# Late stages wholly in program order, and the O*wo stage's loads reordered: wo's last rows first, its third O^T tile ungated

## The chip, the cores and the metric

One core of one Trainium2 chip. The metric is the time of one execution in device microseconds (us). Single executions of one kernel differ by some 20 us here (see the ranges below); in the profiled runs nearly all of that comes from when the attention stage ends. So beside the median of several runs I use a second measure that does not carry that scatter: the **stage start**, the time in one profiled run from row 0's first matmul of the O*wo stage to row 4's first.

## The reference, cut to what matters

```python
def _fwd_reference(A_x, ...):
    xn = _layernorm(A_x)
    s = A(xn, k_cache, v_cache, wq, wo)    # 32 heads of attention, then O @ wo
    g = _silu(B(xn, w_gate, w_up, w_down)) # sigmoid-gated MLP
    return A_x + s * g                     # S = 2048 rows, D = 576

def reference(...):                        # the output and the gradients of all inputs but B_x
    out, vjp = jax.vjp(_fwd_reference, ...)
    return (out, *vjp(grad_out))
```

The product `O @ wo` is the stage that this study is about. It takes some 140 us of 4930.

## The kernel before: the parts that matter

A row block of the stage is 128 rows. Its operand is an O^T tile: SP's transposing load of 128 rows of O for all 32 heads (1.05 MB). Three such tiles are used in turn: `oTs[0]` lies over the attention's KQ, `oTs[1]` over xnT, `oTs[2]` over xn_all. Of wo's rows those of 23 heads (`h_early`) are in SBUF by the time the stage begins; those of nine (`h_late`) go into Kn, Vn and dOn, which the attention uses to its end.

```python
with late("pc") as pc, late("pcf") as pcf, \
        tc.manual_schedule(engines={SP, Pool, DVE, PE}):     # ScalarE is left to the scheduler
    # ...
    def row_loads(st):                    # GpSimd: three loads of 144 KB for row block st
        res = []
        for nm, src in (("dsg", dsg_d), ("g2b", g2_d), ("xb", x2)):
            t_ = ldp3.tile([P, D], bf, name=nm)
            nc.gpsimd.dma_start(t_[:], src[st * P:(st + 1) * P, :])
            res.append(t_)
        return res

    R0 = min(3, NT)
    loads = {}
    loads[0] = row_loads(0)
    for st in range(1, R0):
        if st > 1:                        # the gate: one element of oTs[2] <- row 0's xb
            nc.gpsimd.tensor_copy(oTs[st][0:1, 0, 0:1], loads[0][st % 3][0:1, 0:1])
        load_oT(oTs[st], st)              # SP: dma_start_transpose
    for view, h0, n, dead in wo_parts:
        if dead in (1, 2, 3):
            load_wo_rows(view, h0, 0, n)  # GpSimd: Kn, Vn, dOn, 432 KB each
    for st in range(1, R0):
        loads[st] = row_loads(st)
    # ...
    def close(st):                        # after row block st's last matmul
        accs = accs_of.pop(st)
        dsg, g2b, xb = loads.pop(st)
        if st + R0 < NT:
            load_oT(oTs[st % 3], st + R0)          # SP
            loads[st + R0] = row_loads(st + R0)    # GpSimd: does not wait for SP
        # ... ScalarE: s_sb <- accs; VectorE: doB <- s_sb*dsg, xb <- s_sb*g2b + xb
        nc.gpsimd.dma_start(o0[st * P:(st + 1) * P, :], xb[:])

    for st in range(R0 - 1):
        mm(st, h_early)
    for st in range(NT):
        # ... turn_do: TensorE transposes doB of an earlier row block
        mm(st, h_late if st in accs_of else h_early + h_late)
        close(st)
        if st == 0 and R0 > 1:
            mm(R0 - 1, h_early)
```

Row 3's O^T tile (KQ again) can only be issued when row 0 has closed. Row 3's three loads stand on GpSimd behind those of row 2, and nothing ties them to row 0's close.

## Time and profile before

| | before |
|---|---|
| median of the first three runs (range) | 4933.09 us (4931.61 to 4936.69) |
| profiled run, span | 4929.9 us, mean granted TensorE clock 0.998 |
| TensorE busy | 98% of the span; the chain that ended last is 94% TensorE |
| stage start, 3533.59 to 3577.50 | 43.9 us |
| from row 4's first matmul to the end | 1352.4 us |

The page says that TensorE is the limit, and the timeline says where TensorE stands still. The lines that carry this are in the prediction below. In all views PE is TensorE's matmuls, PEld its weight loads, DVE VectorE, ACT ScalarE, POOL GpSimd and SPq the transfers that SP issues.

### The profile page before, as it was taken

To read this page: it belongs to the slowest core of one execution; us is meant where nothing else is said; L and a number is where in the kernel's file an instruction comes from. 1 tells how busy PE (TensorE), PEld (TensorE's weight loads), DVE (VectorE), ACT (ScalarE), POOL (GpSimd) and SP (SyncE) were. 2 spreads that over 40 slices of the span, in tenths; PEclk is the share of its full clock that TensorE was granted. 3 is DMA by queue.
4 is the path that set the end of the run, shared out by engine and by line. 5 is a ranking of instruction groups with operands and counts; after the bars stand their busy time and mean duration, and the time that the engine had idled before them with its cause. 6 is when DMAs were issued, how large, how long until landed. Compare 5 with 4: busy or idle time off the path is not lost.

```text
span 4929.9 us, 100847 instructions
## 1 busy us (share of the span) xinstructions
PE 4835.4 (98%) x40273; PEld 2894.6 (59%) x41029; DVE 2802.5 (57%) x6554; ACT 2472.1 (50%) x4228; POOL 840.7 (17%) x1329
## 2 busy tenths in 40 slices
PE   9999999999999999999999999999899999999998
PEld 4445666666666666666666666666555555555554
DVE  4544666666666666656656666665434555554215
ACT  4431766766676676666667667667312111111111
POOL 3322111111111111111111111111221111111112
PEclk9999999999999999999999999999999999999999
DMA  7886999999999999999999999999999999998665
GB/s 260 274 201 170 225 227 231 215 227 230 227 232 224 230 227 227 233 221 233 223 224 228 232 226 223 232 229 224 225 221 234 230 232 225 226 224 213 187 173 153
DMA packets 3045845, 1097.11 MB, mean 223 GB/s; under 512 B 2949553, under 2 KB 2953778, under 8 KB 3045362
## 3 DMA queue, kind: packets, MB, share of 16 engines
q1 hardware_dynamic: 2946594, 771.07, 83.5%
q0 software_dynamic: 98160, 318.85, 20.5%
q8 instruction: 323, 5.29, 0.4%
q14 instruction: 160, 1.31, 0.1%
q10 hardware_dynamic: 608, 0.59, 0.0%
HBM read 175.31 MB, written 177.93 MB: 72 GB/s over the span
## 4 chain that ended last, share of the span: by engine, by line
PE 94%; DMA 2%; DVE 2%; issue 1%; ACT 1%; SPq 0%; POOL 0%; POOLq 0%; ACTq 0%; DVEq 0%
PE acc L683 18%; PE acc L744 18%; PE acc L998 13%; PE acc L1054 8%; PE dp L706 8%; PE sp L636 8%; PE acc L215 6%; PE u_ps L450 3%; PE dh L1111 3%; PE g_ps L448 3%; PE acc L533 3%; PE acc L958 2%; PE acct L145 1%; DMA dST<-Pq 1%; DVE Pq L709 1%
## 5 line engine op out<-in xcount | busy, mean ns | idle before, releaser
L654 ACT ACTIVATE Pq<-sp 128x1024 bf16<-128x1024 f32 x1024 | 1047.1, 1023 | 267.3 <-PE sp L636 224.3
L709 DVE SCALAR_TENSOR_TENSOR Pq<-dp,negdelta,Pq 128x1024 bf16<-128x1024 f32 x512 | 655.2, 1280 | 46.6 <-PE dp L706 45.2
L712 ACT ACTIVATE t<-dp,negdelta 128x1024 bf16<-128x1024 f32 x512 | 567.1, 1114 | 214.7 <-PE dp L706 165.3
L683 PEld LDWEIGHTS <-dST 128*128 128x128 bf16 x8192 | 508.2, 98 | 152.1 <-DMA dST<-Pq 11.0
L706 PE MATMUL dp<-VT,dOT 128*128 128x512 bf16 x1919 | 581.6, 379 | 2.4
L683 PEld LDWEIGHTS <-PT 128*128 128x128 bf16 x8192 | 500.1, 98 | 130.9 <-DMA PT<-Pq 11.1
L636 PE MATMUL sp<-KQ 128*128 128x512 bf16 x1858 | 568.9, 380 | 5.2 <-issue 5.2
L683 PE MATMUL acc<-Kn,dST 128*128 128x128 bf16 x8192 | 557.1, 219 | 8.8 <-DMA dST<-Pq 6.9
L683 PE MATMUL acc<-Vn,PT 128*128 128x128 bf16 x8192 | 542.1, 219 | 8.5 <-DMA PT<-Pq 6.2
L744 PE MATMUL acc<-Pq,dOn 128*128 128x512 bf16 x1983 | 527.3, 379 | 10.0
L713 DVE TENSOR_TENSOR Pq<-t,Pq 128x1024 bf16<-128x1024 bf16 x512 | 354.5, 692 | 316.7 <-ACT t L712 306.9
L744 PE MATMUL acc<-Pq,Qn 128*128 128x512 bf16 x2013 | 524.3, 380 | 4.9
L724 ACT ACTIVATE dq_n<-acc,rsc 128x128 bf16<-128x128 f32 x512 | 187.5, 366 | 333.7 <-PE acc L683 312.0
L1154 DVE TENSOR_TENSOR dxn<-acc,dxn 128x576 f32<-128x576 f32 x272 | 206.1, 758 | 247.8 <-PE acc L1054 247.8
L744 PEld LDWEIGHTS <-Qn 128*128 128x128 bf16 x2048 | 200.4, 98 | 240.9 <-issue 1.6
L744 PEld LDWEIGHTS <-dOn 128*128 128x128 bf16 x2048 | 198.8, 98 | 233.8
L1116 ACT ACTIVATE ndh<-dh 128x512 bf16<-128x512 f32 x144 | 86.0, 597 | 452.8 <-DVE du_blk L1114 449.0
L636 PEld LDWEIGHTS <-KQ 128*128 128x128 bf16 x2048 | 179.3, 98 | 127.7 <-issue 7.2
L641 DVE TENSOR_REDUCE rs_all<-rsp 128x1 f32<-128x2 f32 x512 | 78.5, 153 | 306.5 <-ACT Pq L654 295.0
L706 PEld LDWEIGHTS <-dOT 128*128 128x128 bf16 x2048 | 178.8, 98 | 124.4 <-issue 11.9
L677 POOL DMA_DIRECT2D on_d<-o_n x128 | 97.1, 759 | 778.8 <-DVE junk L695 447.8
L677 POOL DMA_DIRECT2D dq_d<-dq_n x128 | 97.9, 765 | 719.7 <-ACT dq_n L724 679.8
(208 smaller groups left out, 6794.4 us busy)
## 6 DMA issues: line engine op xcount, KB each, us to landing
out_dram<-kvn POOLq DMA_DIRECT2D x64, 512.0 KB, 4.7
ah<-a_d POOLq DMA_DIRECT2D x18, 1024.0 KB, 9.2
ah<-h_d POOLq DMA_DIRECT2D x18, 1024.0 KB, 12.1
h_d<-h_row POOLq DMA_DIRECT2D x64, 256.0 KB, 3.5
a_d<-a_row POOLq DMA_DIRECT2D x64, 256.0 KB, 3.8
x_all<-in_A_k_cache_dram SPq DMA_DIRECT2D x64, 256.0 KB, 3.8
on_d<-o_n POOLq DMA_DIRECT2D x128, 128.0 KB, 4.4
kvT_d<-KQ POOLq DMA_DIRECT2D x32, 512.0 KB, 5.3
```

The lines of the kernel that those rows point to most:

```text
L215: nc.tensor.matmul(av[:, :CH], lhsT=w[:, i, :], rhs=srcT[:, i, cs], start=(i == 0), stop=(i == DT - 1))
L636: nc.tensor.matmul(sp[:, c * CH:(c + 1) * CH], lhsT=hs.QT[:, qt * P:(qt + 1) * P], rhs=hs.KT[:, hf * HW_ + c * CH: hf * HW_ + (c + 1) * CH ...
L654: nc.scalar.activation(Pq[:, hsl], sp[:], AF.Exp, scale=SCALE, accum_out=hs.rsp[:, hf:hf + 1])
L683: nc.tensor.matmul(hs.acc[:, 0, :], lhsT=T[:, kt, :], rhs=rhs[:, kt, :], start=(kt == 0), stop=(kt == NT - 1))
L706: nc.tensor.matmul(dp[:, c * CH:(c + 1) * CH], lhsT=hs.dOT[:, qt * P:(qt + 1) * P], rhs=hs.VT[:, hf * HW_ + c * CH: hf * HW_ + (c + 1) * C ...
L709: nc.vector.scalar_tensor_tensor(Pq[:, hsl], dp[:], hs.negdelta[:, qt:qt + 1], Pq[:, hsl], op0=ALU.add, op1=ALU.mult)
L712: nc.scalar.activation(t[:], dp[:], AF.Identity, bias=hs.negdelta[:, qt:qt + 1], scale=1.0)
L713: nc.vector.tensor_tensor(Pq[:, hsl], t[:], Pq[:, hsl], op=ALU.mult)
L744: nc.tensor.matmul(self.acc, lhsT=self.nat[:, qt, :], rhs=self.slabs[qt][:, cs], start=(qt == self.lo), stop=(qt == self.hi - 1))
L998: nc.tensor.matmul(acc[:, n0:n0 + nn], lhsT=lhs[:, st, cols], rhs=rhs[:, st, n0:n0 + nn], start=(st == 0), stop=(st == NT - 1))
L1054: nc.tensor.matmul(acc[:, n0:n0 + nn], lhsT=lT, rhs=w[:, n0:n0 + nn], start=(k == 0), stop=(k == len(terms) - 1))
L1154: nc.vector.tensor_tensor(dxn[:, st, :], acc[:, :D], dxn[:, st, :], op=ALU.add)
```

## The change

Its intent: take away TensorE's three waits at the start of the O*wo stage (7.4 us, and the half clock after them). The copy that gates the transpose into xn_all goes. The last rows of wo are issued ahead of row 0's loads, Kn, whose slab is read longest, as the last of the three. ScalarE, so far left to the scheduler in these stages, runs in program order too.

```diff
-            tc.manual_schedule(engines={SP, Pool, DVE, PE}):      # names shortened
+            tc.manual_schedule():
@@
-            h_late = [h0 + k for _, h0, n, dead in wo_parts if dead in (1, 2, 3) for k in range(n)]
+            h_late = [h0 + k for _, h0, n, dead in sorted(wo_parts, key=lambda w: w[3] == 1) if dead in (1, 2, 3) for k in range(n)]
@@
             loads = {}
-            loads[0] = row_loads(0)
             for st in range(1, R0):
-                if st > 1:
-                    nc.gpsimd.tensor_copy(oTs[st][0:1, 0, 0:1], loads[0][st % 3][0:1, 0:1])
                 load_oT(oTs[st], st)
-            for view, h0, n, dead in wo_parts:
+            for view, h0, n, dead in sorted(wo_parts, key=lambda w: w[3] == 1):
                 if dead in (1, 2, 3):
                     load_wo_rows(view, h0, 0, n)
+            loads[0] = row_loads(0)
             for st in range(1, R0):
                 loads[st] = row_loads(st)
```

## The prediction

> **What bounds the kernel now.** I read the page first: PE (TensorE) is busy 98% of the 4929.9 us, and the chain that ended last is 94% PE. So nothing but TensorE's own gaps, its clock, and the tail after its last matmul can be won. Then I listed what TensorE waited for after 3490 us: its matmuls waited 14.5 us in sum, and about half of that stands in one place, the start of the O*wo stage (L958, 3533 to 3675 us). The third view is the timeline of that start (start us, us, engine and line, what it writes <- reads, count, [idle before <- releaser]):
>
> ```profile
> 3533.59 4.33 PE L958 MATMUL acc<-dsT,KQ 128*128 128x512 bf16 x33
> 3534.85 0.55 POOL L756 DMA_DIRECT2D kvT_d<-VT  x1 [1.81 <-DVE VT L754]
> ...
> 3540.22 0.18 POOL L942 COPY xn_all<-xb 1x1 bf16<-1x1 bf16 x1 [3.21 <-DMA xb<-in_A_x_dram]
> 3540.43 7.27 SPq L584 DMA_TRANSPOSE xn_all<-on_d  x1
> 3540.72 0.76 POOL L575 DMA_DIRECT2D Kn<-in_A_wo_dram  x1 [0.31 <-issue]
> ...
> 3547.80 1.60 PE L958 MATMUL acc<-Kn,KQ 128*128 128x512 bf16 x6 [2.77 <-DMA Kn<-in_A_wo_dram]
> 3547.80 0.10 PEld L958 LDWEIGHTS <-KQ 128*128 128x128 bf16 x1 [2.87 <-issue]
> ...
> 3552.16 0.10 PEld L958 LDWEIGHTS <-KQ 128*128 128x128 bf16 x1 [2.87 <-issue]
> ...
> 3556.34 0.14 PEld L958 LDWEIGHTS <-xn_all 128*128 128x128 bf16 x2 [1.67 <-issue]
> ...
> 3569.38 4.33 PE L958 MATMUL acc<-dsT,KQ 128*128 128x512 bf16 x33
> ...
> 3577.50 2.83 PE L958 MATMUL acc<-dsT,xnT 128*128 128x512 bf16 x20
> ```
>
> A row block of this stage is 32 heads of two matmuls; 23 heads' rows of wo ("early") are already there, 9 ("late": Vn, dOn, Kn) are loaded only now. The order on TensorE is: row 0 early, row 1 early, row 0 late, row 2 early (its O^T tile is xn_all), row 1 late, row 2 late, row 3. The reader should see that SP's transpose into xn_all and GpSimd's wo loads both start only at 3540.4 to 3540.7. The reason is L942, a one-element copy which waits for row 0's xb load. TensorE finishes the two early parts at 3544.9 and then waits three times, 2.87, 2.87 and 1.67 us.
>
> The fourth view is the same stretch in windows (us; then busy time and count of PE, PEld, DVE, ACT, POOL; granted clock, DMA share, GB/s):
>
> ```profile
> 3542.00:3544.00 2.00, 1.95 (x18) 1.04 (x17) 0.00 (x0) 0.00 (x0) 2.00 (x4) 1.00 0.70 133
> 3544.00:3546.00 2.00, 1.03 (x10) 0.48 (x7) 0.00 (x0) 0.00 (x0) 1.66 (x4) 1.00 1.12 242
> ...
> 3548.00:3550.00 2.00, 1.40 (x6) 0.56 (x5) 0.00 (x0) 0.00 (x0) 0.54 (x1) 0.50 1.18 291
> ...
> 3552.00:3554.00 2.00, 1.84 (x8) 0.73 (x8) 0.00 (x0) 0.00 (x0) 0.88 (x2) 0.50 1.14 322
> ...
> 3558.00:3560.00 2.00, 1.78 (x8) 0.80 (x8) 0.20 (x1) 0.00 (x0) 1.51 (x3) 0.50 1.14 248
> ```
>
> The first gap costs twice: the clock falls to 0.50 and stays there to about 3561.
>
> **What the Trainium skill says.** "TensorE: Matmul & The Clock Gate", Part 1 (The HAM clock gate), says that the array runs at half rate after an idle window of about 3.4 us and needs a busy one of that length to come back. The trace agrees on the halving, but a gap of only 2.87 us was enough here, and the second gap kept the clock low for 13 us. "DMA: Bandwidth & Descriptors", Anatomy of one DMA, says that a wait is held by the issuing sequencer, not by the DMA engines; the trace agrees: the three wo loads stand behind L942 on GpSimd. The same page, Issuing engines are not separate DMA queues, says that all queues interleave on the same 16 engines: here the transpose into xn_all, issued with 1.3 MB of wo beside it, took 15.8 us to land, that into xnT just before 7.7. The first page's Architectural detail calls ScalarE strictly first-in-first-out, so its order in the program is the order in which it waits.
>
> **The change part by part.** The order listing of both builds shows that SP and DVE are unchanged, PE only takes Vn, dOn, Kn instead of Kn, Vn, dOn, GpSimd loses the copy and issues the three wo loads before row 0's three, and ScalarE swaps a few neighbours.
>
> Size of the prize. At full clock 23 heads take 5.63 us (3569.38 to 3575.01) and 9 heads with the 0.28 us of one transpose take 2.49 (to 3577.50), so a row is 7.84 and four rows with three transposes are 32.2 us. From 3533.59 to 3577.50 they took 43.9. The loss is 11.7 us: 7.4 of waits and about 4.3 of half clock.
>
> Wo loads. GpSimd's last attention store ends at 3535.4. Before, three row loads (0.55 each), the wait for xb to land, and the copy came between; now Vn is issued at about 3535.5, dOn at 3536.3, Kn at 3537.0: 5.2 us earlier for Vn's place in the queue. Before, the three landed like this (KB, then us from issue to landing):
>
> ```profile
> Kn<-in_A_wo_dram POOLq DMA_DIRECT2D x1, 432.0 KB, 7.0
> Vn<-in_A_wo_dram POOLq DMA_DIRECT2D x1, 432.0 KB, 10.7
> dOn<-in_A_wo_dram POOLq DMA_DIRECT2D x1, 432.0 KB, 11.2
> ```
>
> Transpose into xn_all. Its destination lies on slabs that TensorE reads until its last attention matmuls (3533), and SP is busy with the xnT transpose to 3532.6. So it can start at about 3533, 7.5 us earlier, ahead of the wo loads instead of level with them.
>
> Deadlines, if TensorE never stops: Vn 3544.9, dOn 3545.6, Kn 3546.4, xn_all 3547.1. With latencies unchanged the loads would land at 3542.5, 3547.0 and 3548.2. But half of the transpose is now through before they start. By volume: 1.05 MB of transpose, 0.52 of the kvT store and 1.33 of wo are 2.9 MB, which at 240 GB/s (my estimate from the windows above and the 223 of the page) are 12.1 us; from about 3534.7, when the first of it flows, that ends at 3546.8. So I expect all four to be just in time or some tenths late; a wait of about 1 us in sum, too short to halve the clock. Row 0's dsg now lands after wo, near 3548, but is needed only for the transpose of doB at about 3555.
>
> Next deadline. Row 3's O^T tile is issued when row 0 closes, 3547.1, and needed 41 heads and a transpose later, at 3557.4: 10.3 us, where such transposes into KQ took 9.4 in this stretch. Before, the slow clock gave it 14. Expected wait: some tenths. So 1.2 us of the 11.7 stay, and 10.5 are won.
>
> ScalarE. In the first block of the next stage the fourth negation now comes before the dwd copy; TensorE waited for those negations 0.8 us in the whole trace, so at most tenths. In the last group dqT's second copy moves behind the fourth finishing row's activation (4900.33 + 0.87), so it ends near 4901.8 and TensorE's third dq product, which reuses that accumulator, starts about 0.9 us late. That is not on the path that sets the end:
>
> ```profile
> 4917.75 0.87 ACT L1205 ACTIVATE t<-t,nb,rstd_all 128x576 f32<-128x576 f32 x1 [3.49 <-DVE t L1204]
> 4918.52 0.62 ACT L40 CAST dqT<-acc 128x576 bf16<-128x576 f32 x1
> ...
> 4919.17 1.20 SPq L1246 DMA_TRANSPOSE dwq<-dqT  x1
> ```
>
> The end is set by VectorE's eight finishing rows at 4.36 us each, then the last activation, then dqT; in the new order the last dqT still stands behind the last activation. I book 0. Everything between is TensorE back to back, so what is won at 3577 arrives at the end: 4933.1 - 10.5 = 4922.6.
>
> **Rivals.** (1) The wait moves instead of going: transposes and copies share the engines, and dOn, Kn or xn_all land 2 to 3 us late. For it: "latencies unchanged" gives 1.4 us for dOn and 1.9 for Kn. Against: more than half of the transpose is ahead of them. If one gap reaches the 2.8 us that halved the clock, half of the prize is gone: about 4928. (2) Row 3's tile becomes the wait, as the other rows' loads are now bunched beside it: 2 to 3 us back, 4925. (3) The gain is absorbed later, by loads of the next stage or the tail: 4933. Against: no late group shows TensorE waiting for a load with more than 2 us, and the tail moves with TensorE. (4) ScalarE's order costs on the tail: up to 1 us.
>
> **Range and chances.** Full success without any wait is 4921.4; rivals 1 and 2 together 4930; the three runs before spread from 4931.6 to 4936.7. So 4918 to 4930. A 2% change would be 99 us, eight times the prize, so within 2% is near certain.
>
> **What would show it.** Right: no copy at L942; Vn issued near 3535.5; the transpose into xn_all starts near 3533; granted clock 1.00 from 3536 to 3575; row 4's first matmul near 3567 instead of 3577.5; the last 1350 us unchanged in length. Wrong: a PE wait above 2 us at L958 with clock 0.50 after it (rival 1), or on KQ at row 3 (rival 2), or a stage that ends 10 us earlier with an end that doesn't move (rival 3).

## More of the kernel before

For comparison with the changed kernel, this is the order of transfers around row 3's O^T tile, from the timeline of the kernel before (start us, us on the issuing queue, engine and line, what is written <- read, count, [idle before <- what ended it]; L933 is a row load).

```profile
3554.19 0.54 POOL L933 DMA_DIRECT2D xb<-in_A_x_dram  x1
...
3555.23 4.83 SPq L584 DMA_TRANSPOSE KQ<-on_d  x1
...
3559.03 0.54 POOL L933 DMA_DIRECT2D dsg<-dsg_d  x1
```

The load at 3554.19 is row 3's last. It is issued before the transpose into KQ, which is on SP's queue for 4.83 us; row 4's first load, at 3559.03, comes only after row 0's output store. TensorE does not wait for this tile.

## The result, and the profile after

All ratios here are the mean time of one kernel's fast runs over that of the other's fast runs of the same rounds, so they are not quite the ratio of the medians quoted.

| | before | changed |
|---|---|---|
| median (range) | 4934.89 us (4931.61 to 4938.18), 4 runs | 4932.32 us (4926.75 to 4936.4), 4 runs |
| ratio | | 0.9994, 95% interval 0.9977 to 1.0011 |
| span of the profiled run, clock | 4929.9 us, 0.998 | 4928.9 us, 0.998 |
| stage start | 43.9 us | 44.9 us (3531.67 to 3576.54) |
| from row 4's first matmul to the end | 1352.4 us | 1352.4 us |

The predicted 4922.6 (4918 to 4930) was missed. The time shows no gain, though the interval of these few runs would still allow one of 11 us; the stage start is sharper: it is as long as before (44.9 us against 43.9). The last 1352.4 us are equal, so nothing was won and then lost later. The timeline of the stage start in the changed kernel:

```profile
3531.14 5.46 SPq L584 DMA_TRANSPOSE xn_all<-on_d  x1
...
3533.75 0.75 POOL L575 DMA_DIRECT2D Vn<-in_A_wo_dram  x1 [0.27 <-issue]
...
3545.20 0.90 PE L956 MATMUL acc<-Kn,KQ 128*128 128x512 bf16 x6 [0.36 <-DMA Kn<-in_A_wo_dram]
...
3545.97 0.54 POOL L933 DMA_DIRECT2D xb<-in_A_x_dram  x1
3546.13 11.04 SPq L584 DMA_TRANSPOSE KQ<-on_d  x1
...
3546.50 0.54 POOL L933 DMA_DIRECT2D dsg<-dsg_d  x1
...
3547.56 0.54 POOL L933 DMA_DIRECT2D xb<-in_A_x_dram  x1
...
3564.86 0.54 POOL L933 DMA_DIRECT2D xb<-in_A_x_dram  x1 [13.90 <-DMA out_dram<-xb]
...
3566.21 6.54 PE L956 MATMUL acc<-dsT,KQ 128*128 128x512 bf16 x34 [9.51 <-DMA KQ<-on_d]
```

The upper half is as planned: counted from row 0's first matmul (3531.67), the transpose into xn_all starts 7.4 us earlier than before and the first wo load 5.1 us, and of the waits on wo 0.36 us is left (row 2 begins 14.26 us after row 0 instead of the 13.47 of full-clock rows, 0.8 late in all). The lower half is the loss. The transpose into KQ sits on SP's queue for 11.04 us instead of 4.83, lands 20.1 us after its issue (3546.13 to 3566.21), and TensorE waits 9.51 us for it. The output store beside it is slow too: GpSimd waits 13.90 us for its landing. The new thing in the order is at 3546.50 to 3547.56: row 3's three loads now stand just *behind* the issue of the transpose; before, they stood ahead of it.

The windows of the changed kernel over the same time (us; busy time and count of PE, PEld, DVE, ACT, POOL; granted clock, DMA share, GB/s):

```profile
3546.00:3548.00 2.00, 2.00 (x19) 1.04 (x18) 1.16 (x2) 0.70 (x2) 2.00 (x4) 1.00 0.97 353
3548.00:3550.00 2.00, 2.00 (x19) 1.01 (x16) 1.02 (x2) 0.00 (x0) 0.74 (x3) 1.00 1.06 117
...
3552.00:3554.00 2.00, 2.00 (x21) 1.13 (x19) 0.00 (x0) 0.05 (x1) 0.00 (x0) 1.00 1.32 74
...
3558.00:3560.00 2.00, 0.00 (x0) 0.00 (x0) 1.62 (x3) 0.00 (x0) 0.00 (x0) 1.00 1.16 102
...
3566.00:3568.00 2.00, 1.79 (x7) 0.75 (x8) 0.00 (x0) 0.00 (x0) 0.99 (x2) 0.50 1.27 290
```

Plain loads, all but alone in the first window, moved 353 GB/s. A transpose with nothing beside it starts slowly and then moves 290 (3552.4 to 3554.8 in split_gate below); the last line, where the next transpose is under way, shows the same 290. In between, with both in flight from 3548 to 3562, the engines are as busy (share 1.06 and more) and move 74 to 142. And the idle TensorE drops to half clock, which costs again after the wait. The sum: 32.2 us of work at full clock, 9.9 of waits, and 2.8 left. Of these, 2.2 are the half clock (row 3 took 10.3 us to row 4's first matmul; at full clock it is 8.1); most of the rest is the small delay on wo that the 0.36 does not contain.

So the first question is whether the late KQ is an accident of one run. The second is what in the change makes it late.

### The profile page after: what moved, and what is told of

It reads as the page before. It is cut to its first block, busy times and chain, and to the rows that moved or that the text cites. A ratio compares the mean times of both kernels' runs of the same rounds, so it can differ in the third digit from the quotient of the medians.

```text
span 4928.9 us, 101605 instructions
## 1 busy us (share of the span) xinstructions
PE 4871.4 (99%) x41029; PEld 2892.1 (59%) x41029; DVE 2800.8 (57%) x6554; ACT 2471.6 (50%) x4228; POOL 840.4 (17%) x1328
## 4 chain that ended last, share of the span: by engine, by line
PE 95%; DMA 2%; issue 1%; DVE 1%; ACT 0%; POOL 0%; SPq 0%; POOLq 0%; ACTq 0%; DVEq 0%
PE acc L683 18%; PE acc L744 17%; PE acc L996 13%; PE sp L636 9%; PE dp L706 9%; PE acc L1052 8%; PE acc L215 6%; PE u_ps L450 3%; PE g_ps L448 3%; PE dh L1109 3%; PE acc L533 3%; PE acc L956 2%; PE acct L145 1%; DVE Pq L709 1%; DMA PT<-Pq 1%
## 5 line engine op out<-in xcount | busy, mean ns | idle before, releaser
L636 PE MATMUL sp<-KQ 128*128 128x512 bf16 x2048 | 609.3, 379 | 5.5 <-issue 5.5
L706 PE MATMUL dp<-VT,dOT 128*128 128x512 bf16 x2048 | 609.6, 379 | 2.3
```

The lines of the kernel that those rows point to most:

```text
L636: nc.tensor.matmul(sp[:, c * CH:(c + 1) * CH], lhsT=hs.QT[:, qt * P:(qt + 1) * P], rhs=hs.KT[:, hf * HW_ + c * CH: hf * HW_ + (c + 1) * CH ...
L706: nc.tensor.matmul(dp[:, c * CH:(c + 1) * CH], lhsT=hs.dOT[:, qt * P:(qt + 1) * P], rhs=hs.VT[:, hf * HW_ + c * CH: hf * HW_ + (c + 1) * C ...
```

## The experiments

Kernels are compared only within the same rounds. Every one gave correct results.

### again: the changed kernel once more

No edit.

> The changed kernel itself once more, for a second profile. Theory A (the order of the change makes the wait: row 3's O^T transpose into KQ now runs beside the loads of rows 1 and 2 and lands late): TensorE again waits 6 us or more on KQ before row 3, with the clock at 0.50 after it, and the time is within 3 us of the kernel before. Theory B (chance: transposes and copies sharing the DMA engines slow each other now and then, and the first profile caught one such stretch): the wait on KQ is below 2 us in this profile and row 4's first matmul comes some 10 us after the first profile's place relative to the stage's start, that is 33 to 35 us after row 0's first matmul instead of 44.9.

Measured: 4933.55 us median (4917.48 to 4943.4, 6 runs), ratio 0.9991 (0.9976 to 1.0006). Stage start 46.4 us:

```profile
3578.99 6.29 PE L956 MATMUL acc<-dsT,KQ 128*128 128x512 bf16 x33 [11.90 <-DMA KQ<-on_d]
```

Although its stage began 11 us later than in the first profile, the wait is there again; the transpose had been issued at 3556.53 and took 22.5 us. It belongs to the kernel and not to the run.

### act_only: the kernel before, ScalarE in program order

```diff
-            tc.manual_schedule(engines={SP, Pool, DVE, PE}):
+            tc.manual_schedule():
```

> The kernel before with ScalarE alone put in program order. Both theories: 0 to 1 us from before, the start of the O*wo stage as before (about 43.9 us from row 0's first matmul to row 4's), and about 0.7 us of wait of a dq product for ScalarE's dqT copy in the last group. If ScalarE's order were what eats the gain, this is 5 us or more slower than before.

Measured: 4937.84 us (4929.34 to 4945.38, 6 runs), ratio 1.0009 (0.9995 to 1.0023). Stage start 44.7 us with the waits of before (4.16 on Kn, 2.83 on Vn, 1.15 on xn_all) and none on KQ. The rest took 1358.7 us, 6.3 more than before; 3.27 of that is one wait on ScalarE's dqT copy at 4575. The changed kernel has the same ScalarE order and not that wait: its rest was 1352.4 and 1352.5 us in two profiles. So the order alone does not make it; I found no cause.

### order_only: the changed kernel, ScalarE left to the scheduler

```diff
-            tc.manual_schedule():
+            tc.manual_schedule(engines={SP, Pool, DVE, PE}):
```

> The changed kernel with ScalarE left to the scheduler: the order of the loads alone. Theory A: the same as the changed kernel, a wait on KQ of 6 us or more. Theory B: no such wait in most draws, 8 to 11 us under before. If ScalarE's order cost the gain: clearly faster than the changed kernel.

Measured: 4931.02 us (4930.65 to 4934.12, 5 runs), ratio 0.9997 (0.9984 to 1.001). Stage start 45.5 us, wait on KQ 9.90 us, rest 1352.6. The load order alone does all that the whole change does. ScalarE's order neither won nor cost anything that these runs can show.

### gate_rows: the loads of rows 1, 2 and 3 behind KQ's landing

Row 0's loads stay behind wo; those of rows 1 to 3 are held on GpSimd by a one-element copy that reads the landed KQ tile.

```diff
             loads[0] = row_loads(0)
-            for st in range(1, R0):
-                loads[st] = row_loads(st)
@@ close(st)
                     load_oT(oTs[st % 3], st + R0)
+                    if st == 0:
+                        for r in range(1, R0):
+                            loads[r] = row_loads(r, oTs[0] if r == 1 else None)   # copies one element first
                     loads[st + R0] = row_loads(st + R0)
```

> The changed kernel, with the loads of rows 1 and 2 (and so of row 3) held on GpSimd until the transpose of row 3's O^T into KQ has landed. Theory A: the transpose then runs alone, lands 4 to 6 us after its issue, TensorE waits less than 1 us on KQ, perhaps up to 2 us on the transposes of doB, and the kernel is 8 to 11 us faster than before. Theory B: no better than the repeated changed kernel.

Measured: 4934.53 us (4930.86 to 4943.92, 5 runs), ratio 1.0006 (0.9993 to 1.0019). Stage start 41.4 us:

```profile
3560.25 0.18 POOL L934 COPY dsg<-KQ 1x1 bf16<-1x1 bf16 x1 [16.28 <-DMA KQ<-on_d]
...
3568.32 0.72 PE L914 MATMUL pt<-ident,doB 128*128 128x128 bf16 x5 [5.95 <-DVE doB L971]
```

The transpose was issued at 3552.08, so the tile landed within 8.2 us (to the copy that waited for it), and TensorE did not wait for it. But the gate is too blunt: row 1's dsg now comes late, and TensorE waits 5.95 us for the doB made from it. The wait was moved, not removed; still, it shows that the tile is not issued too late as such.

### split_gate: dsg early, only the rest behind the gate

```diff
             for st in range(1, R0):
-                loads[st] = row_loads(st)
+                loads[st] = row_loads(st, ("dsg",))
@@ close(st)
+                    if st == 0:
+                        for r in range(1, R0):
+                            loads[r] += row_loads(r, ("g2b", "xb"), oTs[0] if r == 1 else None)
                     loads[st + R0] = row_loads(st + R0)
```

> The changed kernel, with the dsg loads of rows 1 and 2 left early (right behind row 0's loads), and only their g2b and xb loads, then row 3's, held on GpSimd until row 3's O^T tile (KQ) has landed. Theory A (the other rows' loads beside it are what makes that tile late): it lands within 6 to 9 us of its issue, no wait of TensorE above 1.5 us on KQ, none above 1.5 us on doB, clock 1.00 through the start of the stage; row 0's first matmul to row 4's first takes 33 to 36 us (before 43.9), and the time is 8 to 11 us under the kernel before: 4922 to 4926. Rival C (the tile is issued too late whatever lies beside it): a wait of 3 us or more on KQ, stage start 38 us or more, time within 5 us of before. Rival D (a wait only moves on, to doB or to xnT of row 4): stage start 37 us or more with that wait named.

Measured: 4926.44 us (4921.99 to 4933.41, 5 runs) against 4933.35 (4924.02 to 4946.72, 11 runs), ratio 0.9983 (0.9967 to 0.9999). Stage start 33.4 us, no wait on row 3's tile, clock 1.00 throughout:

```profile
3549.52 4.58 SPq L584 DMA_TRANSPOSE KQ<-on_d  x1
...
3557.55 0.18 POOL L936 COPY g2b<-KQ 1x1 bf16<-1x1 bf16 x1 [13.43 <-DMA KQ<-on_d]
```

Most of the 11.7 us prize is real and can be had. Rival D was right in a small way: the held loads come out in a burst at 3558 to 3562, and rows 4 and 5 then wait 0.85 and 2.15 us for their tiles. The rest took 1357.3 us instead of 1352.4 in this profile.

### tile4: a fourth O^T tile, issued straight after the third

Row 3's tile goes into a block that is free until row 12; SP issues it at 3540.22, when the xn_all transpose has left its queue, with every row load left as in the changed kernel.

```diff
+            oT_at = {st: oTs[st] for st in range(R0)}
+            oT_at[3] = oT_view(ah0[:].rearrange("p a t f -> p (a t f)"), 0)
-            for st in range(1, R0):
-                load_oT(oTs[st], st)
+            for st in range(1, R0 + 1):
+                load_oT(oT_at[st], st)          # and close(st) loads row st+4 into row st's tile
```

> The changed kernel with a fourth O^T tile, in the block that the next stage's a and h loads use only from row 12 on: row 3's transpose is issued straight after row 2's, near 3537 instead of 3546, with all row loads left where the changed kernel has them. Theory A (transposes and plain copies in flight together are slow, so the engines' time is the scarce thing): no wait on row 3's tile, but wo's last rows or row 2's tile come later, a wait of 2 to 6 us there with half clock after it; stage start 37 to 42 us. Rival C (only the late issue counts): no wait above 1.5 us anywhere, stage start 32.5 to 35 us, time 4921 to 4925.

Measured: 4929.35 us (4919.68 to 4947.96, 6 runs), ratio 0.9994 (0.9974 to 1.0014), so its time tells nothing. Stage start 34.6 us; the only large wait is on the new tile:

```profile
3540.22 12.91 SPq L584 DMA_TRANSPOSE ah<-on_d  x1
...
3562.47 4.34 PE L959 MATMUL acc<-dsT,ah 128*128 128x512 bf16 x34 [2.21 <-DMA ah<-on_d]
```

Theory A fails: wo was not delayed. C is half right: the stage start lies in its 32.5 to 35, but a wait of 2.21 us is left where it had none above 1.5. Counted from row 0's first matmul the transpose was issued some 10 us earlier than in the changed kernel (4.2 us after it instead of 14.5), and it took 22 us to land. So an early issue helps, and most of the advance is eaten up among the other loads. The rate did not collapse here as a whole: 355 GB/s until 3549.5, 176 from there until the tile had landed.

### wo_order and no_gate: two parts of the change alone

On the kernel before, wo_order makes only the sort Vn, dOn, Kn. no_gate makes only this edit:

```diff
-                if st > 1:
-                    nc.gpsimd.tensor_copy(oTs[st][0:1, 0, 0:1], loads[0][st % 3][0:1, 0:1])
```

> The kernel before with one part alone: wo's last rows are loaded and used in the order Vn, dOn, Kn, the copy that gates the transpose into xn_all and the order of row 0's loads left as they were, ScalarE left to the scheduler. All theories: the copy still holds the wo loads, so three waits of 1 to 3 us at the late heads and on xn_all, half clock after them, stage start 43 to 46 us, as before.

> The kernel before with one part alone: the one-element copy is gone, so the second and third O^T tiles are ungated; row 0's three loads still come ahead of wo's last rows. Theory A: the wo loads are issued some 3 us earlier than before and the transpose into xn_all near 3533 to 3537; waits on wo 0 to 2 us; row 3's tile is bunched with the row loads as in the changed kernel, wait on KQ of 6 to 12 us, stage start 43 to 47 us. If the KQ wait comes from loading wo first, it would be below 3 us here and the stage start 34 to 38 us.

Measured, one run each: wo_order 4930.07 us, stage start 43.3 us, waits of 3.70 (Vn), 3.68 (dOn) and 1.16 us (xn_all): as before. no_gate 4941.55 us, but with an attention that ended 10 to 22 us later than in the profiles so far; its stage start is only **32.9 us**, and of a wait on KQ only 0.64 us of the weight load is left. That is the "if" of its expectation that I had not believed. Taking out the gate alone seems to win the whole stage start; the rest of the change seems to lose it again. One profile with such an odd start needed a repetition.

### no_gate2, row0_first: no_gate again, and the change with one part undone

row0_first is the changed kernel with row 0's three loads put back ahead of wo:

```diff
             loads = {}
+            loads[0] = row_loads(0)
@@
                     load_wo_rows(view, h0, 0, n)
-            loads[0] = row_loads(0)
```

> The same kernel as no_gate, again with 5 rounds. Theory E (what ate the gain is that the changed kernel puts row 0's three loads behind wo's last rows: that pushes row 2's loads from just before to just after the start of row 3's transpose, and plain loads among a transpose slow both): as in no_gate, KQ lands 8 to 11 us after issue, no wait on it above 1.5 us, row 0's first matmul to row 4's first takes 32.5 to 34.5 us, time 8 to 11 us under the kernel before, 4922 to 4926. Theory F (no_gate's one profile was a lucky one, its stage began 20 us later than the others'): KQ wait of 5 to 12 us again, stage start 40 to 47 us, time within 4 us of before.

> The changed kernel with one part undone: row 0's three loads stand ahead of wo's last rows again; Vn, dOn, Kn order, no gating copy and ScalarE in program order stay. Theory E: wo lands about 1.6 us later than in the changed kernel and still in time (wait 0 to 1.5 us on Vn, dOn or Kn), KQ wait 0 to 1.5 us, stage start 32.5 to 35 us, time 4922 to 4926. Theory F, or if loading Vn first matters by itself: KQ wait above 5 us, stage start 40 us or more, time within 4 us of before.

A correction to these texts: counting the issues, three a row, the loads that change sides of the transpose are **row 3's**, not row 2's.

Measured against 4938.2 us (4928.67 to 4950.37, 11 runs): no_gate2 4928.95 (4919.91 to 4938.41, 6 runs), ratio 0.9984 (0.9967 to 1.0001), stage start 33.7 us with three waits on wo of 0.33 to 0.37; row0_first 4927.3 (4919.71 to 4937.51, 6 runs), ratio 0.998 (0.9964 to 0.9996), stage start 36.4 us with one wait of 2.39 on Vn and some half clock after it, both more than expected (35 and 1.5 at most). Neither waits for KQ. From the timeline of no_gate2:

```profile
3543.16 0.54 POOL L933 DMA_DIRECT2D dsg<-dsg_d  x1 [0.73 <-DMA Vn<-in_A_wo_dram]
...
3544.42 0.54 POOL L933 DMA_DIRECT2D g2b<-g_d  x1 [0.71 <-DMA dOn<-in_A_wo_dram]
...
3544.95 0.54 POOL L933 DMA_DIRECT2D xb<-in_A_x_dram  x1
3545.11 5.26 SPq L584 DMA_TRANSPOSE KQ<-on_d  x1
...
3555.51 4.33 PE L956 MATMUL acc<-dsT,KQ 128*128 128x512 bf16 x33
```

These three loads are row 3's, and the last is issued 0.16 us *before* the transpose; it leaves SP's queue in 5.26 us and TensorE has no wait at row 3. In the changed kernel they begin 0.37 us *after* it. Theory E holds, theory F falls.

The brackets (and, for the changed kernel, the wait of row 2's g2b at 3545.44 on Kn, which ended after 0.72 us) also show why a move of row 0's loads shifts row 3's. In both timelines the ninth transfer from the kvT store on waits for the first to land, the tenth for the second where that is still under way, and so on: GpSimd keeps eight in flight (what sets the eight I did not test). In no_gate2 the last issue tied to a wo load (dOn, 3544.42) is row 3's second load, so one is left after it. With row 0's loads behind wo, the last one tied to wo (Kn, 3545.44) is row 2's second, and four are left after it, 0.53 us apart. TensorE needs the same wo rows to close row 0, so the transpose is issued about 0.7 us after that tied issue in both kernels, at the far side of row 3's loads in one and in front of them in the other.

### late_rows: no_gate with the loads pushed behind the transpose

```diff
             for st in range(1, R0 - 1):       # was R0: row 2's loads are taken out here
@@ close(st)
-                    loads[st + R0] = row_loads(st + R0)
+                    if st:
+                        loads[st + R0] = row_loads(st + R0)
@@ after the copies into s_sb
+                if st == 0:
+                    loads[R0 - 1] = row_loads(R0 - 1, s_sb)   # one-element copy of s_sb first
+                    loads[R0] = row_loads(R0)
```

> The no_gate kernel with row 2's three loads (and row 3's behind them) held on GpSimd, by a one-element copy that reads row 0's s_sb, until row 0 has closed, so they are issued 0.5 to 3 us after row 3's transpose instead of before it. Nothing else moves and no more bytes flow. Theory E: the transpose into KQ is slow again, 13 us or more from issue to landing, and TensorE waits 3 us or more for KQ; stage start 37 us or more. If the place of row 2's loads does not matter: KQ lands within 11 us, wait below 1.5 us, stage start below 35 us.

Measured, one run: 4937.41 us, stage start 43.3 us:

```profile
3557.96 4.79 SPq L584 DMA_TRANSPOSE KQ<-on_d  x1
...
3559.06 0.54 POOL L935 DMA_DIRECT2D dsg<-dsg_d  x1 [0.31 <-POOL dsg L934]
...
3572.21 4.98 PE L958 MATMUL acc<-dsT,KQ 128*128 128x512 bf16 x20 [3.69 <-DMA KQ<-on_d]
```

With six loads (rows 2 and 3) right behind its issue, the transpose lands after 14.2 us and TensorE waits 3.69 us, although wo is not loaded first here. A wait of 2.92 us on Kn in the same profile belongs to the same 43.3 us, so of the stage start only the KQ part counts for the theory.

### row3_later: the changed kernel with row 3's loads behind the store

```diff
 close(st)
-                    loads[st + R0] = row_loads(st + R0)
+                    if st:
+                        loads[st + R0] = row_loads(st + R0)
@@
                 nc.gpsimd.dma_start(o0[st * P:(st + 1) * P, :], xb[:])
+                if st == 0 and R0 < NT:
+                    loads[R0] = row_loads(R0)
```

> The changed kernel with one line moved: row 3's three loads are issued after row 0's output store instead of before it. (Counted by issues, it is row 3's loads, not row 2's as the expectations of the two calls before say, that stand within 0.4 to 1.4 us behind the start of row 3's transpose in the changed kernel, and before it in no_gate2 and row0_first.) wo still goes first, the same bytes flow, and the same loads follow, only some 3.4 us later. If those three loads at the transpose's start are the whole cause: TensorE waits for KQ under 2 us, stage start (row 0's first matmul to row 4's first) 32.5 to 36 us, time 7 to 11 us under the kernel before. If the wo-first order or the total of bytes in flight is the cause: wait on KQ 5 us or more, stage start 39 us or more, time within 4 us of before. In between: the transpose is hurt by whatever plain load flows beside it, in proportion, wait of 2 to 5 us.

Measured: 4925.87 us (4919.84 to 4931.04, 6 runs) against 4935.09 (4921.42 to 4945.06, 11 runs), ratio 0.9982 (0.9967 to 0.9997). Stage start 34.8 us, the rest 1352.7:

```profile
3545.56 6.62 SPq L584 DMA_TRANSPOSE KQ<-on_d  x1
...
3549.32 0.54 POOL L933 DMA_DIRECT2D dsg<-dsg_d  x1
...
3557.19 4.34 PE L956 MATMUL acc<-dsT,KQ 128*128 128x512 bf16 x33 [1.07 <-DMA KQ<-on_d]
```

With wo still first, only three loads moved from 0.4 to 3.8 us behind the transpose's issue (row 4's first two follow 1.6 us later in consequence): it lands in 11.6 us instead of 20.1, and the wait is 1.07 us instead of 9.51. The bytes are the same: between issue and landing the engines moved some 2.84 MB at 245 GB/s, in the changed kernel some 2.87 MB at 143. The windows still show a slow stretch, but a brief one:

```profile
3548.00:3550.00 2.00, 2.00 (x18) 1.02 (x17) 0.48 (x1) 0.00 (x0) 1.22 (x3) 1.00 1.74 99
...
3552.00:3554.00 2.00, 1.95 (x21) 1.17 (x21) 0.00 (x0) 0.63 (x2) 0.00 (x0) 1.00 1.25 317
```

### All together

| kernel | row 3's loads | KQ from issue to TensorE's use | wait on KQ | stage start |
|---|---|---|---|---|
| before | last 1.04 us before the transpose | 14.2, no wait | 0 | 43.9 (waits on wo) |
| no_gate, no_gate2 | last 0.16 us before | 11.0, then 10.4 without a wait | 0.6 (weight load), 0 | 32.9, 33.7 |
| row0_first | last 0.84 us before | 10.4, no wait | 0 | 36.4 |
| changed, again, order_only | first 0.4 us after | 20.1, 22.5, 20.5 | 9.5, 11.9, 9.9 | 44.9, 46.4, 45.5 |
| late_rows | row 2's and 3's, first 1.1 us after | 14.2 | 3.7 | 43.3 |
| row3_later | first 3.8 us after | 11.6 | 1.1 | 34.8 |
| split_gate, gate_rows | none until it has landed | landed in 8.0, 8.2 | 0 | 33.4, 41.4 |

split_gate, row0_first and row3_later are each faster than the kernel before, by ratios of 0.9983, 0.998 and 0.9982 whose intervals end below 1 (split_gate's at 0.9999). That is 8 to 10 us of 4935, about what the stage start gains in row0_first and row3_later (7.5 and 9.1 us). The repeats of the changed kernel stand at 0.9991 to 0.9997 of before, so these are the versions that beat both, though they and the changed kernel are compared only through the kernel before.

## Why the prediction was wrong

**The prize: right.** 11.7 us were there: 33.4, 33.7 and 34.8 us of stage start were reached by experiments, against the 32.2 worked out from full-clock rows.

**wo and xn_all just in time: right.** Predicted about 1 us of waits; measured 0.36 on Kn and 0.8 of delay in all, clock 1.00 until the wait for KQ.

**"Next deadline": the step that failed.** The prediction said that row 3's O^T tile has 10.3 us, "where such transposes into KQ took 9.4 in this stretch", and "Expected wait: some tenths". It measured 20.1 us and a wait of 9.51. The 9.4 is moreover one landing only, that of row 6's tile (issued at 3577.42 in the kernel before); for row 3's tile that trace has no landing, only the 14.2 us to its use. In that kernel row 3's loads had been issued ahead of the transpose, and two of row 6's three ahead of row 6's. I carried the figure over without asking what the change puts beside it. The order listing showed GpSimd's issues in their new order, and the timeline of before showed on which landings they wait. From the two one can count that four loads instead of one are left after the last wo landing. I counted bytes and deadlines for wo and xn_all only.

**Rival 2 had the place, nearly the cause, and the wrong size:** "Row 3's tile becomes the wait, as the other rows' loads are now bunched beside it: 2 to 3 us back, 4925". The size was wrong by the same term. I let extra bytes cost their share of 240 GB/s; 0.44 MB would be 1.8 us. But the rate is not constant: it fell to 143 GB/s over the 20 us, where the same bytes flowed at 245 in row3_later. The prediction's own example gave no sign of this: beside 1.3 MB of wo the transpose into xn_all took 15.8 us at 220 GB/s, so there it was indeed more bytes. (The 7.7 us that it sets against this is not the transpose "just before" but row 4's, issued at 3566.82.)

**The half clock** then returned, as the prediction's own "what would show it wrong" has it: a wait above 2 us on KQ with 0.50 after it.

**Rival 3 fell:** the remaining 1352.4 us did not change. **ScalarE booked at 0** stands as far as 0.1% can be seen: order_only and again do not differ (0.9997 and 0.9991). That ScalarE waits in program order, which the prediction took from the skill, no run here tests by itself.

**Which part of the change did what.** Removing the gate (no_gate, no_gate2) wins 10 to 11 us of stage start; no_gate2's time agrees, but its interval just reaches 1.0001. Sorting Vn first alone (wo_order, one run) does nothing. Loading wo before row 0's rows was meant to help and costs most of that again; undoing it (row0_first) or moving row 3's loads (row3_later) restores the gain.

**What stays open:** why transposing and plain packets together ran at a third of the rate here and not in other stretches (220 GB/s beside wo in the kernel before, 355 for 9.5 us in tile4), and why loads at the head of a transpose hurt so much more than 3.8 us into it. The traces show the rates and not the cause. Each stage start is one profile; only the changed load order was profiled three times (44.9 to 46.4). late_rows, with twice the loads but 0.7 us later, was hurt less (14.2 us against 20.1), so the relation is not a simple one.

## What to carry to other kernels

When a change moves transfers earlier, follow the queue to its end: find what used to be issued before the next critical transfer and is now issued behind it, and count issues, not only bytes. Do not carry a transfer's landing time over from a trace in which other neighbours flowed beside it; here a 1.05 MB transpose took 8 us alone, 20 us with three small loads at its head, and 11.6 us with the same loads 3.8 us later. Test the parts of a change one by one even where the whole shows nothing: here one part won 10 us of stage start and another lost most of them.

## What the Trainium skill lacked or had wrong

- "DMA: Bandwidth & Descriptors", Rules for kernel authors, says of correctness that a transpose next to ordinary DMAs "needs nothing". For time that is not so here: 8.0 us to land alone, 20.1 us with row loads, a store and the next loads in flight. No page that I found gives the rate of a transpose mixed with plain copies, or says that mixing can cost more than the bytes: 2 us windows with both showed 74 to 142 GB/s for 14 us at a DMA share above 1 in the changed kernel (not everywhere: 220 beside wo in the kernel before), and moving three loads of unchanged size took the landing from 20.1 to 11.6 us.
- "Advanced Engine Details and Errata", X-Bar Transpose (TRN2), says that transposing DMAs are as fast as regular ones and expects 350 to 400 GB/s. Here a transpose with nothing beside it moved 290 GB/s at its steadiest (2.4 us in split_gate) and 1.05 MB in 8.0 us as a whole; a 2 us window with plain loads almost alone moved 353.
- No page that I found says that GpSimd holds its ninth transfer until the first of the eight before it has landed, as the timelines here show: for example 3.32 us of such a wait on the kvT store in the changed kernel, 5.71 in late_rows. Whether the chip or this program sets the eight, no run here shows.
- "TensorE: Matmul & The Clock Gate", Part 1, ties half clock to an idle window of about 3.4 us. Shorter gaps were enough here: row0_first's 2.39 us on Vn was followed by a 4 us window at 0.67, the 2.87 us of the kernel before by one at 0.50. Gaps of 2.21 us in tile4 and 2.15 in split_gate left it at 1.00.
